# Gated mix of two attention blocks: all PSUM banks in one tile, with joined exponentials and row maxima and an own order per pair of key tiles

## The chip, the core and the metric

The kernel runs on one core of a Trainium2 chip. Its engines work side by side: TensorE (PE) multiplies matrices into PSUM, which has eight banks of 128 x 512 f32; VectorE (DVE) and ScalarE (ACT) read PSUM and write SBUF; GpSimd (POOL) works in SBUF; SyncE (SP) issues DMAs. Each engine runs its own instructions in order and waits for others through semaphores: each engine has a count that its finished instructions raise, and a wait names a count that has to be reached. The metric is the time of one execution on the device in microseconds, lower is better; before it is 2671.39 us, the median of three runs.

## The reference

Two attention blocks over the same x (2048 tokens, 576 features, 32 heads of 18) are mixed by a sigmoid gate. Block A has its own keys and values for each head, block B one key and one value head for all:

```python
g = sigmoid((x * gate_w).sum(-1, keepdims=True))
a = softmax(qA @ kA.T * 18**-0.5) @ vA @ A_wo        # per head, 32 heads
b = softmax(qB @ kB.T * 18**-0.5) @ vB @ B_wo        # one k, v for 32 heads
out = g * a + (1 - g) * b
```

B's query and key weights are drawn eight times larger than the others, so its scores are large and the row maxima are needed.

## The kernel before

There are 64 heads in all (`NU`, 32 of B, then 32 of A). A first stage projects x into queries, keys and values and parks them in DRAM; the values are still projected while the first maxima run. The main stage walks over `NSTEP` = 1024 steps, a step being one tile of 128 rows of one head, two steps (a **pair**) a turn of the loop over `T`, eight pairs a head.

Three streams run at once, at different places of the walk:

- **Maxima**, 22 steps ahead (`LEAD`). `step_max` multiplies 128 query rows with 512 keys (one chunk `c` of four) into a PSUM bank, and DVE takes the row maximum (L524). Chunks 0 and 1 share one DVE pass: a product with the difference of the two key chunks (`x`) goes through a Relu on ACT into SBUF (L518), and a custom DVE instruction adds it to chunk 0's product and takes the maximum (L521). So a step has four matmuls, three DVE passes and one ACT pass. `max_rows` gathers the maxima of a head and puts them into two more rows of the queries, through which the next product subtracts them.
- **Scores** at `T`. `step_scores` multiplies 128 keys with 512 queries (four chunks a step) into a bank, and ACT takes the exponential into an SBUF tile (L560).
- **PV**, one or two steps behind. `step_pv` multiplies the exponentials with the values, four chunks on four column groups, and adds up in the bank `acc` over 16 steps (L566), whole (512 columns) or in two halves of 256. `head_out` copies `acc` out once a head (L588).

The operands of scores lie in partitions 0 to 55, those of maxima and `x` in 64 to 117, so that two matmuls can be in the array at once.

PSUM is in three pools: four banks for scores and `x` (`ps_s`), three for maxima (`ps_m`), one for `acc`. Each call of a pool's `tile` gives the next buffer, and the framework makes a matmul wait for whoever read the buffer last. The exponentials have a pool of 12 buffers of 128 x 512.

The order on PE is written by hand: strings of operations, one for each pair, chosen by the place in the head (`PLAIN`, `END`, `AFTER`, `BEFORE_ROWS`, `ROWS`) and by whether a unit of the output projection is due (`UNIT`, `UNIT_END`, `UNIT2`). `mB1` is the maximum of the second step's chunk 1, `sA0` the score of the first step's chunk 0, `x` the difference product, `P` and `Q` a whole PV step, `p f` and `h H` its halves, `U` a unit (12 matmuls and an addition into `oacc`, L695 and L703). The order on ACT and DVE follows from it, since each consumer is recorded right behind its matmul. A turn of the loop:

```python
for op in order.split():
    k, second, c = op[0], op[1:2] == "B", op[2:]
    ...
    elif k in "mM":
        step_max(*divmod(M + second, 16), int(c), k == "M", T < 0 and c == "3")
    elif k == "s":
        ...
```

DMAs are issued beside this by SP, from generators (`normalise`, `prep_wo`, `out_proj`) that are pulled once a turn.

Of the kernel before, what the change touches and what calls it, by code (L numbers as in the profile page):

```python
# [19 lines left out]
S = 2048  # L20
D = 576
H = 32
# [27 lines left out]
def gated_mix_kernel(ctx: ExitStack, tc: tile.TileContext, xT, wall, wv, wo, out):  # L50
# [34 lines left out]
    ones_r = dram.tile([2, S], F16, name="ones_r")  # L85
    acc = ps_o.tile([P, 512], F32, name="acc")

    def other():
        return ps_s.tile([P, 512], F32, name="ps")

# [150 lines left out]
    def bank(odd=False):  # L241
        return ps_m.tile([P, 512], F32, name="pm") if odd else ps_s.tile([P, 512], F32, name="ps")

# [50 lines left out]
    def project_v(st_, hf, w):  # L294
        fp = ps_s.tile([P, 512], F32, name="ps")
# [206 lines left out]

    def step_max(u, i, c, low=False, spare=False):

# [7 lines left out]
        else:  # L512
            k = kst(u)[b:b + 54, c * 512:(c + 1) * 512]
        pm = other() if c == "x" or spare else ps_m.tile([P, 512], F32, name="pm")
        nc.tensor.matmul(pm, qs[u % 3][b:b + 54, i * P:(i + 1) * P], k, start=True, stop=True)  # L515
        if c == "x":
            MX["x", u, i] = lead.tile([P, 512], F32, name="xb", bufs=2)
            nc.scalar.activation(MX["x", u, i], pm, AF.Relu)  # L518
        elif c == 0 and ("x", u, i) in MX:
            junk = lead.tile([P, 512], BF16, name="junk", bufs=1)  # L520
            nc.vector.tensor_tensor_reduce(junk, pm, MX.pop(("x", u, i)), 1.0, -3e38, op0=OP.add, op1=OP.max,  # L521
                                           accum_out=MX[u][:, i, c:c + 1])
        else:
            nc.vector.tensor_reduce(MX[u][:, i, c:c + 1], pm, axis=AX.X, op=OP.max)  # L524
# [20 lines left out]

    def step_scores(u, i, c, alone, x=None):

        x = c if x is None else x
        b = SB
        ps = (ps_m if alone and c == 0 else ps_s).tile([P, 512], F32, name="pm" if alone and c == 0 else "ps")  # L550
        if alone and c % 2:
            b = MB
        nc.tensor.matmul(ps, kst(u)[b:b + 56, i * P:(i + 1) * P],  # L553
                         qs[u % 3][b:b + 56, x * 512:(x + 1) * 512], start=True, stop=True)
        PT["q"] = PT.get("q", []) + [(x, ps)]
        if alone and c == 0:
            return
        for c, ps in PT.pop("q"):
            pt = L["pt"].tile([P, 512], F32, name="pt")
            nc.scalar.activation(pt, ps, AF.Exp, scale=SCALE / LIFT ** 2)  # L560
            PT[u, i, c] = pt

# [105 lines left out]
    def out_proj(t0, rows, first=False):  # L668
# [15 lines left out]
        for q in range(8):  # L684
# [3 lines left out]
            for s2 in range(2):  # L688
                st_ = 2 * q + s2
                for hf in range(2):  # L690
                    fp = ps_m.tile([P, 512], F32, name="pm")
                    n = 0
# [23 lines left out]

    def end_bank(n=[0]):
        n[0] += 1
        return ps_s.tile([P, 512], F32, name="ps") if n[0] % 7 < 4 else ps_m.tile([P, 512], F32, name="pm")

    def last_half(h):
# [10 lines left out]
        yield  # L732
        pt = ps_m.tile([P, 512], F32, name="pm")[:, 0:256]
        for c in range(2):
# [7 lines left out]
        yield  # L742
        pb = ps_m.tile([P, 512], F32, name="pm")[:, 0:256]
        for c in range(2):
# [7 lines left out]
    def end_bank(n=[0]):  # L752
        n[0] += 1
        return ps_s.tile([P, 512], F32, name="ps") if n[0] % 7 < 4 else ps_m.tile([P, 512], F32, name="pm")

    def last_units():

        w = WO[8]
        for n in range(32):
            st_, hf = divmod(n, 2)  # L760
            end = END_T[st_ // 8]
            fp = end_bank() if n > 1 else ps_m.tile([P, 512], F32, name="pm")
            for m, (a, b) in enumerate(PRODS):
# [67 lines left out]

    FIRST = "sA0 mA2 sA1 mA0 sA2 mA3 sA3 mB0 sB0 mB1 sB1 mB2 sB2 mB3 sB3 x"
    PLAIN = "mB1 mB3 sA0 sA1 mA3 sA2 P mB2 sA3 x sB0 mA2 sB1 mB0 h sB2 mA0 H sB3"
    UNIT = "mB2 sA0 mB0 sA1 mA0 P mB3 sA2 mA2 sA3 Q mA3 sB0 x sB1 mB1 sB2 U sB3"
    END = "mB2 sA0 mB3 mB1 sA1 p sA2 mA2 sA3 mA0 sB0 f x mB0 sB1 mA3 sB2 Q sB3"
    AFTER = "mB1 mA3 sA0 sA1 sA2 mA0 P sA3 mA2 sB0 mB2 x sB1 mB0 h sB2 mB3 H sB3"
    BEFORE_ROWS = "mA0 sA0 mB3 sA1 mB1 sA2 p sA3 mA2 f sB0 mB2 sB1 mB0 x sB2 mA3 Q sB3"
    ROWS = "mB3 sA0 mA3 sA1 mB1 sA2 P mB2 sA3 sB0 mA0 x sB1 mB0 h sB2 mA2 H sB3"
    UNIT_END = "mB3 sA0 mA2 sA1 mA3 sA2 P sA3 mB1 sB0 mB2 Q x sB1 mA0 sB2 mB0 sB3 U"
    UNIT2 = "sA0 mA3 sA1 mB0 sA2 P sA3 mB1 sB0 mB2 sB1 x U mA2 sB2 mA0 sB3 Q mB3"  # L840
    ALONE = "sA0 sA1 P U sA2 sA3 U sB0 sB1 h U sB2 sB3 H U"
# [4 lines left out]
    LAST_U = (TL + 14,)  # L846
    LEADS = "mA0 MA1 mA2 MA3 V.A mB0 MB1 mB2 MB3 V.B"
    order = None
    TAIL = {TL: [N8], TL + 2: [N8], TL + 6: [N8, N8, N8], TL + 8: [HALF[0]], TL + 10: [N8]}
    for T in range(-LEAD, NSTEP + 2, 2):  # L850
# [9 lines left out]
        order = LEADS if T < 0 else FIRST if T == 0 else LAST if T > TL else ALONE if alone else (UNIT2 if T >= SEG[1][3] else UNIT_END if T % 16 == 0 else UNIT) if units else \  # L860
            {0: END, 2: AFTER if T > 2 else PLAIN, 8: BEFORE_ROWS, 10: ROWS}.get(T % 16, PLAIN)
        for op in order.split():
# [87 lines left out]
```

## Time and profile before

| what | us |
|---|---|
| median of three runs | 2671.39 |
| lowest and highest | 2669.41, 2672.8 |
| span of the profiled execution, first to last instruction | 2669.7 |
| busy: PE, DVE, ACT, POOL | 2652.4, 2421.4, 2393.3, 283.8 |

The profiled execution has no time of its own beside its span; the median of the runs lies 1.7 us above that span. Busy is the time in which at least one instruction of the engine is under way. A matmul's row begins when it starts and ends when its last result is in PSUM, while the next one starts earlier, so a busy PE need not be at its peak. Rows of the profile name line, engine, operation, output and input, and the count; in brackets stands how long the engine was idle before, and who ended that.

### The profile page before, as it was taken

How to read it: one execution, taken by the hardware profiler on the slowest of the kernel's cores; microseconds unless marked ns; L12 is line 12 of the kernel's file. 1: busy time of each engine (PE TensorE's matmuls, PEld its weight loads, DVE VectorE, ACT ScalarE, POOL GpSimd, SP SyncE). 2: the span in 40 equal slices, each digit the busy share in tenths (PEclk: the TensorE clock that was granted, in tenths of full speed). 3: DMA queues.
4: the chain of work that ended last, by engine and by line, in shares of the span. 5: the costliest groups of instructions: out<-in, count | busy, mean ns of one | idle time of the engine just before them, and what ended most of it. 6: DMA issues, size and time to landing. Idle time of an engine off the chain costs nothing.

```text
span 2669.7 us, 58607 instructions
## 1 busy us (share of the span) xinstructions
PE 2652.4 (99%) x22278; PEld 898.0 (34%) x22278; DVE 2421.4 (91%) x4588; ACT 2393.3 (90%) x4814; POOL 283.8 (11%) x526
## 2 busy tenths in 40 slices
PE   9999999999999999999999999999999999999998
PEld 7778322222222222222222222222222222223444
DVE  8447999999999999999999999999999999998873
ACT  4341899999999999999999999999999999998875
POOL 4740000001001100100110002000200011001000
PEclk9999999999999999999999999999999999999999
DMA  7332000011001100210132112112121212122312
GB/s 202 125 112 76 23 20 20 20 37 40 28 17 46 44 20 18 54 33 20 36 77 82 43 53 85 43 55 59 58 67 51 55 54 61 40 70 86 90 36 95
DMA packets 127304, 150.15 MB, mean 56 GB/s; under 512 B 55456, under 2 KB 94744, under 8 KB 125933
## 3 DMA queue, kind: packets, MB, share of 16 engines
q1 hardware_dynamic: 112593, 119.38, 15.7%
q0 software_dynamic: 8096, 19.30, 2.1%
q10 hardware_dynamic: 6332, 7.71, 0.8%
q8 instruction: 175, 2.87, 0.4%
q14 instruction: 108, 0.88, 0.1%
HBM read 90.80 MB, written 46.45 MB: 51 GB/s over the span
## 4 chain that ended last, share of the span: by engine, by line
PE 93%; DVE 5%; ACT 1%; DMA 1%; issue 1%; SPq 0%; ACTq 0%; DVEq 0%
PE acc L566 38%; PE ps L553 26%; PE pm L515 13%; PE pm L695 4%; PE ps L515 4%; PE ps L248 3%; PE pm L248 3%; DVE mx L524 2%; PE ps L297 2%; DVE junk L521 0%; ACT pt L560 0%; DVE norm_a L190 0%; DVE pl L262 0%; DMA R<-r_d 0%; DVE oacc L772 0%
## 5 line engine op out<-in xcount | busy, mean ns | idle before, releaser
L560 ACT ACTIVATE pt<-ps 128x512 f32<-128x512 f32 x4074 | 2105.6, 651 | 63.1 <-PE ps L553 51.5
L524 DVE TENSOR_REDUCE mx<-pm 128x1 f32<-128x512 f32 x3072 | 1914.1, 682 | 68.0 <-PE pm L515 34.0
L553 PE MATMUL ps<-qs,ksb 56*128 56x512 f16 x2688 | 807.3, 380 | 0.0
L515 PE MATMUL pm<-ksb,qs 54*128 54x512 f16 x2341 | 762.5, 380 | 1.1 <-DVE mx L524 0.6
L566 PE MATMUL acc<-pt,vb 128*19 128x256 f32 (+1 forms) x6144 | 592.4, 457 | 0.0
L566 PE MATMUL acc<-pt,vg 128*19 128x256 f32 (+1 forms) x5496 | 561.7, 480 | 0.3
L515 PEld LDWEIGHTS <-qs 54*128 54x128 f16 x4096 | 293.1, 94 | 516.1 <-issue 455.4
L553 PE MATMUL ps<-qs,ksa 56*128 56x512 f16 x1386 | 407.5, 380 | 0.3
L515 PE MATMUL pm<-ksa,qs 54*128 54x512 f16 x1232 | 399.8, 380 | 1.6 <-DVE mx L524 1.1
L553 PEld LDWEIGHTS <-ksb 56*128 56x128 f16 x2688 | 202.4, 93 | 487.5 <-issue 446.3
L521 DVE CUSTOM_DVE_ANT_0 junk<-pm,xb 128x512 bf16<-128x512 f32 x501 | 341.0, 681 | 9.4 <-PE pm L515 9.0
L518 ACT ACTIVATE xb<-ps 128x512 f32<-128x512 f32 x501 | 319.6, 638 | 7.7 <-PE ps L553 7.3
L534 POOL TENSOR_SCALAR mt<-mt 128x32 f32<-128x32 f32 x64 | 18.6, 290 | 1626.4 <-DVE mt L532 1626.4
L553 PEld LDWEIGHTS <-ksa 56*128 56x128 f16 x1408 | 100.6, 94 | 233.1 <-issue 213.5
L566 PEld LDWEIGHTS acc<-pt,vb 128*19 128x19 f32 x6144 | 104.3, 97 | 216.1 <-issue 208.6
L566 PEld LDWEIGHTS acc<-pt,vg 128*19 128x19 f32 x5496 | 93.2, 97 | 213.1 <-issue 209.7
L515 PE MATMUL ps<-kdb,qs 54*128 54x512 f16 x373 | 140.5, 377 | 0.1
L300 ACT ACTIVATE vst<-ps 128x288 f32<-128x288 f32 x32 | 13.2, 412 | 60.6 <-PE ps L297 60.6
L256 ACT ACTIVATE ph<-ps,tv 128x512 f16<-128x512 f32 x29 | 19.8, 687 | 49.3 <-PE ps L248 34.3
L256 ACT ACTIVATE ph<-pm,tv 128x512 f16<-128x512 f32 x27 | 18.3, 687 | 48.0 <-PE pm L248 29.4
L703 DVE TENSOR_TENSOR oacc<-pm,oacc 128x288 f32<-128x288 f32 x32 | 14.6, 457 | 46.0 <-PE pm L695 45.9
L262 DVE SCALAR_TENSOR_TENSOR pl<-pm,tv,ph 128x512 f16<-128x512 f32 x27 | 20.0, 748 | 37.5 <-ACT ph L256 24.5
(167 smaller groups left out, 1544.6 us busy)
## 6 DMA issues: line engine op xcount, KB each, us to landing
qs<-qkh SPq DMA_DIRECT2D x244, 72.0 KB
qs<-qkl SPq DMA_DIRECT2D x122, 72.0 KB
onh<-oh SPq DMA_DIRECT2D x32, 256.0 KB
onl<-ol SPq DMA_DIRECT2D x32, 256.0 KB
oih<-onh SPq DMA_DIRECT2D x16, 512.0 KB
oil<-onl SPq DMA_DIRECT2D x16, 512.0 KB
ot<-oe SPq DMA_DIRECT2D x220, 36.0 KB
qkh<-ph POOLq DMA_DIRECT2D x56, 128.0 KB, 2.1
```

The costliest lines, as they stand in the source:

```text
L248: nc.tensor.matmul(fp[:, a0:b0], w[a][:kr, k, :], X[b][:kr, k, s0 + a0:s0 + b0], start=(n == 0), stop=(n == len(PROJ) - 1), skip_group_che ...
L256: nc.scalar.activation(h, fp, AF.Copy, scale=t)
L262: nc.vector.scalar_tensor_tensor(l, fp, t, h, op0=OP.mult, op1=OP.subtract)
L297: nc.tensor.matmul(fp[:, 0:288], X[b][:kr, k, st_ * P:(st_ + 1) * P], w[a][:kr, k, :], start=(n == 0), stop=(n == len(PROJ) - 1))
L515: nc.tensor.matmul(pm, qs[u % 3][b:b + 54, i * P:(i + 1) * P], k, start=True, stop=True)
L518: nc.scalar.activation(MX["x", u, i], pm, AF.Relu)
L521: nc.vector.tensor_tensor_reduce(junk, pm, MX.pop(("x", u, i)), 1.0, -3e38, op0=OP.add, op1=OP.max, accum_out=MX[u][:, i, c:c + 1])
L524: nc.vector.tensor_reduce(MX[u][:, i, c:c + 1], pm, axis=AX.X, op=OP.max)
L553: nc.tensor.matmul(ps, kst(u)[b:b + 56, i * P:(i + 1) * P], qs[u % 3][b:b + 56, x * 512:(x + 1) * 512], start=True, stop=True)
L560: nc.scalar.activation(pt, ps, AF.Exp, scale=SCALE / LIFT ** 2)
L566: nc.tensor.matmul(acc[32 * j:32 * j + 19, a:b], v_of(u, i), PT[u, i, j][:, a:b], start=(i == 0 and a == 0), stop=(i == 15), skip_group_ch ...
L695: nc.tensor.matmul(fp[:, 0:288], o[b][:r, t, s2 * P:(s2 + 1) * P], w[a][:r, t, 288 * hf:288 * hf + 288], start=(n == 0), stop=(n == 3 * nt ...
```

## The change

PSUM becomes a single tile `bk` of eight banks. Two counters stand for the pools: `next_s` gives banks 0 to 3 in turn, `next_m` banks 4 to 6; `acc` is bank 7. The exponentials get one tile of 16 slots. A score that is held (`S` in the orders means: take this score's exponential together with the one before) is not given to ACT at once, and one ACTIVATE then reads two banks and writes two slots; of two maxima where the second is marked `N`, one DVE reduce reads two banks and writes two numbers. Where the two banks don't follow each other, the access takes them with a stride, in ascending order, as 0 and 3. The strings now name eight scores, six maxima, one chunk 0 (`c`) and one `x` a pair, with `p0` and `p1` for the two PV steps and `h` and `f` for a half and a whole, and there is one string for each of a head's eight pairs. Pairs with a unit have the same strings with `U` at the end. The turns ahead of `T` = 0 and behind the last maximum keep their old strings.

```diff
-    ps_s = ctx.enter_context(tc.tile_pool(name="ps_s", bufs=4, space=PSUM))
-    ps_m = ctx.enter_context(tc.tile_pool(name="ps_m", bufs=3, space=PSUM))
-    ps_o = ctx.enter_context(tc.tile_pool(name="ps_o", bufs=1, space=PSUM))
+    ps = ctx.enter_context(tc.tile_pool(name="ps", bufs=1, space=PSUM))
...
+    bk = ps.tile([P, 8, 512], F32, name="bk")
+    acc = bk[:, 7, :]
+    RING = {"s": 0, "m": 0}
+
+    def next_s():
+        RING["s"] += 1
+        return (RING["s"] - 1) % 4
+
+    def next_m():
+        RING["m"] += 1
+        return 4 + (RING["m"] - 1) % 3
...
-        L["pt"] = ctx.enter_context(tc.tile_pool(name="ppool", bufs=12, side="left"))
+        L["pt"] = ctx.enter_context(tc.tile_pool(name="ppool", bufs=1, side="left")).tile([P, 16, 512], F32, name="pt")
...
+        elif join == "first":
+            MX["j"] = (n, 4 * i + c)
+        elif join == "second":
+            (n0, c0), (n1, c1) = sorted((MX.pop("j"), (n, 4 * i + c)))
+            flat = MX[u].rearrange("p i c -> p (i c)")
+            nc.vector.tensor_reduce(flat[:, c0:c1 + 1:c1 - c0], bk[:, n0:n1 + 1:n1 - n0, :], axis=AX.X, op=OP.max)
...
+    def exps(q):
+
+        q = sorted(q, key=lambda e: e[0])
+        t = next_pt(len(q))
+        n = [e[0] for e in q]
+        if len(q) == 1:
+            o, i = L["pt"][:, t[0], :], bk[:, n[0], :]
+        else:
+            o, i = L["pt"][:, t[0]:t[1] + 1:t[1] - t[0], :], bk[:, n[0]:n[1] + 1:n[1] - n[0], :]
+        nc.scalar.activation(o, i, AF.Exp, scale=SCALE / LIFT ** 2)
...
-    PLAIN = "mB1 mB3 sA0 sA1 mA3 sA2 P mB2 sA3 x sB0 mA2 sB1 mB0 h sB2 mA0 H sB3"
...
-    AFTER = "mB1 mA3 sA0 sA1 sA2 mA0 P sA3 mA2 sB0 mB2 x sB1 mB0 h sB2 mB3 H sB3"
...
+    PLAIN = ("s c m x s N S p0h m s p0h m s m s S N s p1f",
+             "m s s N S s m p0f x s c S m p1h s m m s p1h",
+             "m s s m p0h x s c s s m p0h m S N s p1h s m p1h",
+             "s m m s S m s p0f s c m s m S p1h s m x p1h",
+             "s m m s S N s p0h s m p0h c s s m N S x p1f",
+             "s m s N S s m p0f s m x s m N S p1h s c p1h",
+             "m s m s m s p0h x s m s p0h s c S m m s p1f",
+             "m s m x s S N p0h c s p0h m s s m S m s p1f")
...
+        for n, op in enumerate(ops):
+            if op in "sS":
+                k = ns.index(n)
+                step_scores(*divmod(T + k // 4, 16), k % 4, hold=k < 7 and ops[ns[k + 1]] == "S")
```

What stands on PE at the start of a head's second pair. Names are tile and operand, `ps` a score's or an `x`'s bank, `pm` a maximum's, `bk` any bank of the new tile, and the bracket names the engine whose count is waited for. Before, L553 is a score, L515 a maximum, L566 PV:

```order
L515 LDWEIGHTS qs_94
L515 MATMUL pm<-ksb,qs_94 128x512 [waits DVE_49]
L553 LDWEIGHTS ksb
L553 MATMUL ps<-qs_93,ksb 128x512 [waits Activation_49]
L553 LDWEIGHTS ksb
L553 MATMUL ps<-qs_93,ksb 128x512 [waits Activation_49]
L553 LDWEIGHTS ksb
L553 MATMUL ps<-qs_93,ksb 128x512 [waits Activation_49]
L515 LDWEIGHTS qs_94
L515 MATMUL pm<-ksb,qs_94 128x512 [waits DVE_49]
L566 MATMUL acc<-pt,vb 19x512 [waits DVE_49]
L566 MATMUL acc<-pt,vb 19x512 x3
```

and after, where L588 is a score, L527 a maximum and L603 PV, from the pair's second score (held, bank 3) over its joined score (bank 0) and the next one (bank 1) to PV:

```order
L588 LDWEIGHTS ksb
L588 MATMUL bk<-qs_87,ksb 128x512
L527 LDWEIGHTS qs_88
L527 MATMUL bk<-ksb,qs_88 128x512 [waits DVE_49]
L588 LDWEIGHTS ksb
L588 MATMUL bk<-qs_87,ksb 128x512
L588 LDWEIGHTS ksb
L588 MATMUL bk<-qs_87,ksb 128x512 [waits Activation_49]
L527 LDWEIGHTS qs_88
L527 MATMUL bk<-ksb,qs_88 128x512
L603 MATMUL bk<-pt,vb 19x512 [waits DVE_49]
L603 MATMUL bk<-pt,vb 19x512 x3
```

followed, behind that PV step, by:

```order
L527 LDWEIGHTS qs_88
L527 MATMUL bk<-kdb,qs_88 128x512
L588 LDWEIGHTS ksb
L588 MATMUL bk<-qs_87,ksb 128x512
L527 LDWEIGHTS qs_88
L527 MATMUL bk<-ksb,qs_88 128x512 [waits DVE_49]
L588 LDWEIGHTS ksb
L588 MATMUL bk<-qs_87,ksb 128x512
L527 LDWEIGHTS qs_88
L527 MATMUL bk<-ksb,qs_88 128x512
```

Before, each score waits for ACT by itself. After, the scores into banks 3 and 0 carry no wait; the one into bank 1 does, ahead of PV; of the later matmuls the `x` (bank 2) and the scores into banks 3 and 0 carry none again.

On ACT, around the same pair, L560 and L518 of before are an exponential and an `x`'s Relu:

```order
L518 ACTIVATE xb<-ps 128x512 [waits DVE_49,PE_49]
L560 ACTIVATE pt<-ps 128x512 [waits PE_49] x8
L518 ACTIVATE xb<-ps 128x512 [waits DVE_49,PE_49]
L560 ACTIVATE pt<-ps 128x512 [waits PE_49] x7
L518 ACTIVATE xb<-ps 128x512 [waits DVE_49,PE_49]
```

and after, L577 and L530 are those:

```order
L577 ACTIVATE pt<-bk 128x512 [waits PE_49,Activation_49]
L577 ACTIVATE pt<-bk 128x1024 [waits PE_49,Activation_49]
L577 ACTIVATE pt<-bk 128x512 [waits PE_49]
L530 ACTIVATE xb<-bk 128x512 [waits DVE_49,PE_49]
L577 ACTIVATE pt<-bk 128x1024 [waits PE_49,Activation_49]
L577 ACTIVATE pt<-bk 128x512 [waits PE_49]
L577 ACTIVATE pt<-bk 128x512 [waits PE_49,Activation_49] x3
L530 ACTIVATE xb<-bk 128x512 [waits DVE_49,PE_49]
```

Seven or eight exponentials between two Relus were as many instructions, with one wait each; in the piece of after two instructions write 1024 columns, and several also wait for ACT's own count, for the older exponential in the same slots.

More of the change, by code (lines that the diff above doesn't have):

```diff
@@ L294, in project_v @@
     def project_v(st_, hf, w):
-        fp = ps_s.tile([P, 512], F32, name="ps")
+        fp = other()
         for n, (a, b, k, kr) in enumerate(PROJ):
@@ L501, in gated_mix_kernel, with step_max @@
     MX = {}
-    def step_max(u, i, c, low=False, spare=False):
+    def step_max(u, i, c, low=False, spare=False, join=None):
         if u not in MX:
@@ L847, in gated_mix_kernel, with steps_pair @@
     LEADS = "mA0 MA1 mA2 MA3 V.A mB0 MB1 mB2 MB3 V.B"
+    def steps_pair(T, M, order, units):
+        ops = order.split()
+        ns = [n for n, op in enumerate(ops) if op in "sS"]
+        nm = [n for n, op in enumerate(ops) if op in "mN"]
+        ncm = [n for n, op in enumerate(ops) if op == "c"]
+        maxima = [(0, c) for c in range(2, 4)] + [(1, c) for c in range(4)]
+        assert len(ns) == 8 and len(nm) == 6 and len(ncm) == 1
+        which = {}
+        for k, n in enumerate(nm):
+            which[n] = maxima[k]
+        ring = RING["m"]
+        at_bank = {}
+        for n, op in enumerate(ops):
+            if op in "mNcU":
+                at_bank[n] = ring % 3
+                ring += 1
+        joined = {n for k, n in enumerate(nm) if k + 1 < len(nm) and ops[nm[k + 1]] == "N"}
+        for k, n in enumerate(nm):
+            if ops[n] == "N" and at_bank[nm[k - 1]] > at_bank[n]:
+                which[n], which[nm[k - 1]] = which[nm[k - 1]], which[n]
+        for n, op in enumerate(ops):
+            if op in "sS":
+                k = ns.index(n)
+                step_scores(*divmod(T + k // 4, 16), k % 4, hold=k < 7 and ops[ns[k + 1]] == "S")
+            elif op in "mN":
+                e, c = which[n]
+                step_max(*divmod(M + e, 16), c, join="second" if op == "N" else "first" if n in joined else None)
+            elif op == "c":
+                step_max(*divmod(M, 16), 0)
+            elif op == "x":
+                if M + 2 < NSTEP:
+                    step_max(*divmod(M + 2, 16), "x")
+            elif op == "U":
+                pull(1)
+            elif T >= 2:
+                k, h = int(op[1]), op[2]
+                part = PART.get(k, 0)
+                PART[k] = part + (256 if h == "h" else 512)
+                step_pv(*divmod(T - 2 + k, 16), part, PART[k])
+                if PART[k] == 512:
+                    del PART[k]
+                    if k == 1 and T % 16 == 0:
+                        head_out(T // 16 - 1)
+    PART = {}
     order = None
```

70 lines of the change are left out of this document (40 added, 30 removed), and 7 rows, old and new, of the table UNIT2.

## The prediction

> **What bounds the kernel now.** I read the page first, then the copies that end each head, then one head's stretch, then its chain. The page's span, its busy line and its chain by engine:
>
> ```profile
> span 2669.7 us, 58607 instructions
> PE 2652.4 (99%) x22278; PEld 898.0 (34%) x22278; DVE 2421.4 (91%) x4588; ACT 2393.3 (90%) x4814; POOL 283.8 (11%) x526
> PE 93%; DVE 5%; ACT 1%; DMA 1%; issue 1%; SPq 0%; ACTq 0%; DVEq 0%
> ```
>
> PE carries the chain. The copy of the accumulator (L588) runs once a head; three answers on its line (count, least/median/most ns, first and last start) give the period of a head in three parts of the program, and one stretch of a head's length shows the engines:
>
> ```profile
> L588 DVE COPY oe<-acc x28: 680/681/682, 316.4 to 1277.4; 128x512 f32<-128x512 f32 x28
> L588 DVE COPY oe<-acc x22: 681/686/686, 1456.0 to 2250.0; 128x512 f32<-128x512 f32 x22
> L588 DVE COPY oe<-acc x4: 684/685/686, 2430.3 to 2569.9; 128x512 f32<-128x512 f32 x4
> 387.50:423.00 35.50, 35.50 (x322) 9.12 (x320) 35.13 (x68) 35.46 (x73) 0.75 (x3) 1.00 0.07 19
> ```
>
> A plain head takes (1277.4 - 316.4) / 27 = 35.59 us, a head with projection units 794.0 / 21 = 37.81, one of the last 139.6 / 3 = 46.53. In the stretch PE, DVE (35.13) and ACT (35.46) are all full, so what PE must do and what it waits for have to be told apart. The chain of waits, piece by piece (start, length), does that:
>
> ```profile
> 423.43 0.21 PE ps L553
> 423.64 0.20 PE pm L515
> 423.84 0.01 PE ps L553
> 423.85 0.98 PE acc L566 x8
> 424.84 0.32 PE ps L553
> 425.16 0.00 PE pm L515
> 425.16 0.21 PE ps L553
> ...
> 425.93 0.56 PE acc L566 x8
> 426.49 0.32 PE ps L553
> 426.80 0.01 PE pm L515
> 426.81 0.56 PE acc L566 x8
> ```
>
> A score and a maximum on different rows of the array run side by side and cost one slot of 0.215 us, 0.32 behind a PV group; a whole PV step costs 0.98, a half 0.56. A head of before has 24 groups of 72 slots (each string gone through, two of the same kind taking two slots), 16 halves, 8 wholes: 24 x 0.32 + 48 x 0.215 + 16 x 0.56 + 8 x 0.98 = 34.8 us. PE waits 0.8 us a head, no more: it is the bound, with the two others close behind.
>
> **The change, part by part: the work.** The new strings have 25 groups, 70 slots, 18 halves and 7 wholes: 8.0 + 45 x 0.215 + 18 x 0.56 + 7 x 0.98 = 34.62 us of PE, 0.18 less. For ACT and DVE, the spacing of single instructions and what 512 more elements cost:
>
> ```profile
> 1000.25 4.03 ACT L560 ACTIVATE pt<-ps 128x512 f32<-128x512 f32 x8
> 437.32 2.48 DVE L524 TENSOR_REDUCE mx<-pm 128x1 f32<-128x512 f32 x4
> L136 ACT ACTIVATE wh<-wst 128x512 fp32r<-128x512 f32 x14 | 8.7, 624 | 3.9 <-DMA wst<-wall 3.9
> L339 ACT ACTIVATE xh<-xs 128x1024 fp32r<-128x1024 f32 x8 | 8.4, 1056 | 0.5 <-DMA xs<-xT 0.4
> L177 DVE TENSOR_REDUCE norm_b<-wst 128x1 f32<-128x512 f32 x3 | 2.0, 673 | 0.0
> L177 DVE TENSOR_REDUCE norm_b<-wst 128x1 f32<-128x312 f32 x1 | 0.5, 459 | 0.0
> L560 ACTq EVENT_SEMAPHORE  x31: 17/17/17, 350.1 to 1418.2; - x31
> ```
>
> Exponentials follow each other at (4.03 - 0.65) / 7 = 0.48 us; a second bank adds 1056 - 624 = 432 ns, so a joined pair takes 0.91 instead of 0.96. Not shown is a read of two PSUM banks: the second could cost from 0.43 (this row) to 0.48 (a whole one more); I take 0.43, the only row of that length. 14 joins a head save up to 0.7 us of ACT. Against it, an exponential that also waits for an older one needs a separate wait of 17 ns; the built program has 756 more, 12 a head, 0.2 us. Reduces follow at (2.48 - 0.68) / 3 = 0.60, a second bank adds 512 x 214 / 200 = 548 ns, so a join saves 0.05; the built program has 9 a head, 0.5 us. None of this is on PE. If PE were free of new waits, a head would take between 34.62 and, with the 0.8 us of waits kept, 35.4 us.
>
> **The waits.** All of PSUM is one tile now, and the built program takes a strided access as covering everything between its ends. A join of banks 0 and 3 counts as touching 1 and 2. In the second pair of a head (the PE rows shown with the change) the ring stands so that the held score and the one joined to it fill banks 3 and 0; the next score, bank 1, waits for ACT's count 1408, and the instruction that raises it to 1408 is the exponential of 0 and 3. Bank 1's own reader stood two instructions earlier. The later rows agree: the matmuls into banks 2, 3 and 0 carry no wait, though the join has just read 3 and 0, since that one wait covers them. Of 875 joined exponentials 375, six a head, are 0 with 3; of 562 joined maxima 196, three a head, are 4 with 6, and the next matmul into bank 5 waits for them alike. PE is in order, so all behind the waiting matmul stands still, PV steps too.
>
> The price comes from three delays of before: a matmul to the exponential that waits for it, an exponential's length, and its end to the matmul that waits (the same for a reduce):
>
> ```profile
> 583.21 0.39 PE L553 MATMUL ps<-qs,ksb 56*128 56x512 f16 x1
> 583.63 1.08 ACT L560 ACTIVATE pt<-ps 128x512 f32<-128x512 f32 x2 [0.16 <-PE pm L515]
> 276.29 0.60 ACT L560 ACTIVATE pt<-ps 128x512 f32<-128x512 f32 x1 [0.40 <-PE pm L515]
> 276.94 0.37 PE L553 MATMUL ps<-qs,ksb 56*128 56x512 f16 x1
> 275.83 0.69 DVE L524 TENSOR_REDUCE mx<-pm 128x1 f32<-128x512 f32 x1 [0.35 <-PE pm L515]
> 276.58 0.37 PE L515 MATMUL pm<-ksb,qs 54*128 54x512 f16 x1 [0.17 <-DVE mx L524]
> ```
>
> That is 0.42, 0.60 and 276.94 - 276.89 = 0.05. From the start of the score that completes a join to the start of the score that waits for it at least 0.42 + (0.60 + 0.43) + 0.05 = 1.50 us pass. In four of the six places the waiting matmul is the next slot, 0.215 after: 1.28 us lost each, 5.14 in all. In one a slot and a half PV step lie between, 0.215 + 0.32 + 0.56 = 1.10, lost 0.40; in one a half PV step, 0.88, lost 0.62. Sum 6.16 us a head. For a join of 4 and 6 it is 0.42 + 0.69 + 0.55 + 0.06 = 1.72; over the nine places, less what lies between and what an exponential's wait covers already, 3 x 0.84 + 0.62 + 0.21 + 0.22 = 3.57, and a third of them in each head falls on 4 and 6: 1.2 us. Its bounds are 0, if those waits fall under others, and 3 x 0.84 = 2.5.
>
> PE's head becomes 34.62 + 6.16 + 1.2 = 41.98. Of the 0.8 us of old waits I keep half, 0.4, since ACT and DVE now have some 8 us a head to catch up in: 42.4, or 6.8 us over 35.59. Its ends: 40.8 with no DVE waits and no old ones, 44.3 with the old ones whole and each join begun 0.25 us late behind an ACT still at work (6 x 0.25). Joins occur from the second pair on until the maxima end, 500 pairs or 62.5 heads; I take the same loss in heads with units, where PE has the same strings and the unit on top. 62.5 x 6.8 = 425 us, on the span 2669.7: 3095. The runs' median is 1.7 us above that execution's span: **3096 us**. The larger ring of exponentials costs and hides nothing: PV reads two pairs behind, and its rows have no wait on ACT.
>
> **Rivals.** *The other side: the bank waits are already met.* If the exponential of 0 and 3 ended before PE came to bank 1, only the smaller work would count: 34.62 to 35.4 us a head, 62.5 x -0.2 to -1.0, that is 2610 to 2660, say 2640. For it: all three engines have less to do. Against it: the waited-for exponential cannot begin until the score just ahead of the waiting one is done; it turns only where over 1.28 us of PE work lies between those two, and in four of six places none does.
>
> *The clock falls.* Two pauses of 1.28 us lie 1.7 us apart, at the end of the fifth pair of a head and in the sixth. The windows (PE busy, ..., granted clock, DMA share, GB/s) show two falls of before:
>
> ```profile
> 66.00:70.00 4.00, 2.49 (x12) 1.77 (x11) 3.39 (x8) 0.00 (x0) 2.88 (x4) 1.00 0.29 98
> 72.00:75.00 3.00, 3.00 (x9) 2.37 (x9) 1.41 (x2) 1.12 (x2) 1.93 (x4) 0.58 0.23 79
> 276.00:279.00 3.00, 2.62 (x12) 0.81 (x10) 3.00 (x7) 2.71 (x6) 0.00 (x0) 1.00 0.20 66
> 279.00:283.00 4.00, 3.96 (x17) 0.69 (x17) 2.92 (x5) 3.28 (x7) 0.00 (x0) 0.57 0.00 0
> ```
>
> With PE busy 2.49 of 4 us, and 2.62 of 3, the clock fell to a half for some (1 - 0.57) / 0.5 x 4 = 3.4 us. Of a new head of 42.4 us about 29 are matmuls at work (70 slots of 0.215, 16 PV steps less their change-over), two thirds; at half speed a spell loses about 3.4 / 2 x 0.68 = 1.15 us. Once a head: 62.5 x 1.15 = 72 us, 3168; three times, 3310. Against it: by far the most of a head has pauses further apart than these two. [...]
>
> *Half the price.* If only the exponentials' waits bit and the old waits vanished, 40.8 us a head: 62.5 x 5.2 = 325, 2996. This is the low end of the forecast.
>
> *The change does not join what it says.* The built program has 875 and 562 joins over 62.5 heads: it does.
>
> **How the numbers follow.** Forecast, full clock, 2996 to 3215 (44.3 us a head): 0.74. Clock falls, 3168 and up: 0.14. Waits already met, 2610 to 2660: 0.06. Something cancels the waits to within a measurement: 0.02. Slower by under 300 us through a cause I don't see: 0.04. From 2980 to 3240 lies the forecast and half of the clock case, 0.81. A measurement of this kernel tells some 0.2% from no change: faster 0.06, same 0.02, slower 0.92.
>
> **What would show it.** Right: the accumulator copies stand 41 to 44 us apart; in the second pair of a head a score starts 1.5 us behind the one before it, 0.05 behind a joined exponential of some 1.03 us; the same twice in the fifth to sixth and in the eighth pair; ACT's and DVE's busy shares fall under 85% and exponentials wait for PE; places that join neighbouring banks show none of it. Wrong: heads of 35 us or less, or scores into bank 1 that start beside the joined exponential; a granted clock under 1.0 within the heads would be the clock's case.

## The result and the profile after

The changed kernel takes 3259.22 us (median of four runs, 3256.24 to 3261.41), 1.2205 times the time of before, 95% interval [1.2187, 1.2222]. That is 163 us more than predicted and 19 over the range's upper end. The page of its profiled execution, span, busy line and chain by engine:

```profile
span 3254.5 us, 59842 instructions
PE 2805.2 (86%) x23238; PEld 967.0 (30%) x23238; DVE 2448.0 (75%) x4026; ACT 2423.9 (74%) x3939; POOL 282.8 (9%) x526
PE 61%; ACT 23%; DVE 12%; issue 3%; DMA 0%; POOL 0%; SPq 0%; ACTq 0%; DVEq 0%; POOLq 0%
```

No engine is full any more, and ACT and DVE, which had 1% and 5% of the chain, hold 35%: the engines wait for each other in turn. The copies that end a head (now L625; count, least/median/most ns, first and last start) of the plain heads, of the heads with units and of three of the last:

```profile
L625 DVE COPY oe<-bk x32: 691/692/693, 332.9 to 1712.6; 128x512 f32<-128x512 f32 x32
L625 DVE COPY oe<-bk x21: 691/692/694, 1756.8 to 2709.4; 128x512 f32<-128x512 f32 x21
L625 DVE COPY oe<-bk x4: 691/691/692, 2974.6 to 3149.0; 128x512 f32<-128x512 f32 x4
```

A plain head takes 1379.7 / 31 = 44.51 us (35.59 before), one with units 952.6 / 20 = 47.63 (37.81), one of the last 58.1 (46.53). The chain of waits (start, length), at the place in the head's second pair of which the prediction spoke:

```profile
1000.15 0.02 PE bk L588
1000.17 0.02 issue
1000.19 0.02 ACTq L577
1000.21 0.04 issue
1000.25 0.38 ACT pt L577
1000.63 0.11 issue
1000.75 1.03 ACT pt L577
1001.77 0.04 issue
1001.82 0.37 PE bk L588
```

The held score and its partner are done; ACT first takes an earlier exponential (1000.25), then the joined one (1000.75, 1.03 us), and 0.05 us behind its end the score into bank 1 starts. Six places of that head as the timeline has them, the bracket being how long PE stood idle and for whom, with the row of the joined score (the second of two) first; two are in the second pair, one is a joined maximum's, two lie at the fifth and sixth pairs, one in the eighth:

```profile
999.99 0.59 PE L588 MATMUL bk<-qs,ksb 56*128 56x512 f16 x2
...
1001.82 0.37 PE L588 MATMUL bk<-qs,ksb 56*128 56x512 f16 x1 [1.23 <-ACT pt L577]
...
1005.11 0.37 PE L588 MATMUL bk<-qs,ksb 56*128 56x512 f16 x1 [0.61 <-ACT pt L577]
...
1010.67 0.37 PE L527 MATMUL bk<-ksb,qs 54*128 54x512 f16 x1 [0.44 <-DVE mx L540]
...
1020.44 0.37 PE L527 MATMUL bk<-kdb,qs 54*128 54x512 f16 x1 [1.13 <-ACT pt L577]
...
1023.78 0.37 PE L588 MATMUL bk<-qs,ksb 56*128 56x512 f16 x1 [1.23 <-ACT pt L577]
...
1042.44 0.37 PE L588 MATMUL bk<-qs,ksb 56*128 56x512 f16 x1 [1.26 <-ACT pt L577]
```

The joined score starts at 999.99 + 0.59 - 0.37 = 1000.21, so 1.61 us pass to the waiting one where the prediction had 1.50. The list of waits sums them (us in total, times, longest):

```profile
PE bk L588 <- ACT pt L577: 292.5, 287, 2.3
PE bk L527 <- ACT pt L577: 71.1, 62, 1.2
PE bk L527 <- DVE mx L540: 69.1, 118, 1.3
```

and the groups by form have the joined instructions (busy us, mean ns):

```profile
L577 ACT ACTIVATE pt<-bk 128x1024 f32<-128x1024 f32 x875 | 898.8, 1027 | 4.1 <-PE bk L588 3.3 <-PE bk L527 0.3
L540 DVE TENSOR_REDUCE mx<-bk 128x2 f32<-128x1024 f32 x562 | 685.7, 1220 | 122.4 <-PE bk L527 118.5 <-PE bk L588 1.6
```

The rows with ACT as the releaser count 349 waits, which is close to the 375 strided joins. A joined exponential lasts 1.03 us and a joined reduce 1.22, as worked out (1.03 and 0.69 + 0.55 = 1.24). The strided read itself is hardly slower: the shortest of the 875 joined exponentials lasts 1017 ns, so with a mean of 1027 the 375 strided ones among them last at most 1.04 us in the mean; and the 366 joined reduces of e1 below, all of neighbouring banks, last 1214 ns in the mean, against 1220 here with 196 strided ones among 562.

### The profile page after: what moved, and what is told of

The parts are those of the page before. It is cut to its first block, busy times and chain, and to the rows that moved or that the text cites. A ratio compares the mean times of both kernels' runs of the same rounds, so it can differ in the third digit from the quotient of the medians.

```text
span 3254.5 us, 59842 instructions
## 1 busy us (share of the span) xinstructions
PE 2805.2 (86%) x23238; PEld 967.0 (30%) x23238; DVE 2448.0 (75%) x4026; ACT 2423.9 (74%) x3939; POOL 282.8 (9%) x526
## 4 chain that ended last, share of the span: by engine, by line
PE 61%; ACT 23%; DVE 12%; issue 3%; DMA 0%; POOL 0%; SPq 0%; ACTq 0%; DVEq 0%; POOLq 0%
PE bk L603 24%; ACT pt L577 20%; PE bk L527 14%; PE bk L588 12%; PE bk L259 5%; DVE mx L542 4%; DVE mx L540 4%; PE bk L732 4%; ACT xb L530 2%; DVE junk L533 2%; PE bk L308 2%; DVE sm L654 0%; DVE oacc L805 0%; PE bk L797 0%; SPq L56 0%
## 5 line engine op out<-in xcount | busy, mean ns | idle before, releaser
L577 ACT ACTIVATE pt<-bk 128x512 f32<-128x512 f32 (+1 forms) x3221 | 2103.6, 720 | 465.4 <-PE bk L588 274.1
L542 DVE TENSOR_REDUCE mx<-bk 128x1 f32<-128x512 f32 x1970 | 1264.9, 684 | 261.8 <-PE bk L527 191.0
L588 PE MATMUL bk<-qs,ksb 56*128 56x512 f16 x2688 | 826.5, 387 | 193.6 <-ACT pt L577 193.6
L527 PE MATMUL bk<-ksb,qs 54*128 54x512 f16 x2363 | 746.8, 386 | 46.9 <-DVE mx L540 45.8
L540 DVE TENSOR_REDUCE mx<-bk 128x2 f32<-128x1024 f32 x562 | 685.7, 1220 | 122.4 <-PE bk L527 118.5
L603 PE MATMUL bk<-pt,vb 128*19 128x256 f32 (+1 forms) x6400 | 617.2, 458 | 0.2 <-PE bk L527 0.2
L603 PE MATMUL bk<-pt,vg 128*19 128x256 f32 (+1 forms) x6200 | 592.2, 454 | 0.0
L527 PEld LDWEIGHTS <-qs 54*128 54x128 f16 x4096 | 288.4, 94 | 748.2 <-issue 687.9
L588 PE MATMUL bk<-qs,ksa 56*128 56x512 f16 x1408 | 419.2, 384 | 99.2 <-ACT pt L577 98.9
L533 DVE CUSTOM_DVE_ANT_0 junk<-bk,xb 128x512 bf16<-128x512 f32 x501 | 345.8, 690 | 129.5 <-PE bk L588 80.4
L527 PE MATMUL bk<-ksa,qs 54*128 54x512 f16 x1232 | 392.8, 382 | 23.6 <-DVE mx L540 23.3
L530 ACT ACTIVATE xb<-bk 128x512 f32<-128x512 f32 x501 | 300.2, 599 | 80.8 <-PE bk L527 49.3
L588 PEld LDWEIGHTS <-ksb 56*128 56x128 f16 x2688 | 205.0, 94 | 425.0 <-issue 360.7
L603 PEld LDWEIGHTS bk<-pt,vb 128*19 128x19 f32 x6400 | 109.2, 97 | 397.4 <-issue 396.7
L603 PEld LDWEIGHTS bk<-pt,vg 128*19 128x19 f32 x6200 | 105.5, 97 | 374.2 <-issue 373.9
L527 PE MATMUL bk<-kdb,qs 54*128 54x512 f16 x373 | 143.6, 385 | 52.8 <-ACT pt L577 52.8
L588 PEld LDWEIGHTS <-ksa 56*128 56x128 f16 x1408 | 103.8, 94 | 213.4 <-issue 174.8
L625 DVE COPY oe<-bk 128x512 f32<-128x512 f32 x63 | 43.6, 692 | 102.2 <-PE bk L603 102.2
```

The lines of the kernel that those rows point to most:

```text
L540: nc.vector.tensor_reduce(flat[:, c0:c1 + 1:c1 - c0], bk[:, n0:n1 + 1:n1 - n0, :], axis=AX.X, op=OP.max)
L577: nc.scalar.activation(o, i, AF.Exp, scale=SCALE / LIFT ** 2)
L588: nc.tensor.matmul(bk[:, n, :], kst(u)[b:b + 56, i * P:(i + 1) * P], qs[u % 3][b:b + 56, x * 512:(x + 1) * 512], start=True, stop=True)
L603: nc.tensor.matmul(acc[32 * j:32 * j + 19, a:b], v_of(u, i), PT[u, i, j][:, a:b], start=(i == 0 and a == 0), stop=(i == 15), skip_group_ch ...
L625: nc.vector.tensor_copy(oe, acc)
```

## The experiments

"W" is the prediction's cause: the framework takes an access over banks 0 and 3 (or 4 and 6) as one that covers the banks between, and PE waits for the joined reader. All times have the kernel before, run beside them on the same chip, as the base of the ratio.

**e1: joins of neighbouring banks alone.** The strings, tile and rings stay; a pair that isn't in neighbouring banks is read by two single instructions.

```diff
+            if n1 - n0 > 1:
+                for b0, f0 in (j, (n, 4 * i + c)):
+                    nc.vector.tensor_reduce(flat[:, f0:f0 + 1], bk[:, b0, :], axis=AX.X, op=OP.max)
+            else:
...
-        if alone:
+        if alone or len(q) == 2 and abs(q[0][0] - q[1][0]) > 1:
```

> The changed kernel, but a held score whose banks are 0 and 3, and a pair of maxima in banks 4 and 6, are read one bank at a time; 500 of 875 exponentials and 366 of 562 maxima stay joined. Theory W (a joined access over banks that don't touch is taken to cover the banks between, and PE waits for it): nothing is left to wait for, a plain head takes 35 to 35.6 us, the clock stays full, 2640 to 2720 us in all. Rival J (a read of two banks is itself what costs, by holding two banks to its end): 500 + 366 of 1437 joins are left, so some 60% of the 588 us stay, about 3020. Rival O (the order of the strings costs): no change, about 3250.

Measured: 2691.45 us, ratio 1.0079 [1.0062, 1.0096]. Its busy line, and the copies of its plain heads:

```profile
PE 2668.0 (99%) x23238; PEld 954.8 (35%) x23238; DVE 2388.7 (89%) x4222; ACT 2372.0 (88%) x4314; POOL 283.4 (11%) x526
```

```profile
L630 DVE COPY oe<-bk x32: 678/679/681, 322.6 to 1425.0; 128x512 f32<-128x512 f32 x32
```

Its chain by line from 1000 to 1040 us, and all of PE's waits for DVE's maxima:

```profile
by line: PE bk L608 48.1%; PE bk L527 29.8%; PE bk L593 22.8%
```

```profile
PE bk L527 <- DVE mx L545: 1.5, 8, 0.2
PE bk L527 <- DVE mx L547: 1.1, 4, 0.5
```

Of the 588 us that the change lost (3259.22 - 2671.25, before in the same runs), 568 go with the strided joins. A plain head is 1102.4 / 31 = 35.56 us, and its chain is PE and nothing else. 500 joined exponentials and 366 joined maxima are still there, so joining and holding a score cost nothing to speak of where the banks are neighbours.

**e2: only the strided exponentials undone**, so that the 196 strided maxima remain.

```diff
-        if alone:
+        if alone or len(q) == 2 and abs(q[0][0] - q[1][0]) > 1:
```

> The changed kernel with the exponentials of banks 0 and 3 read one bank at a time, the maxima of banks 4 and 6 still joined (196 of them, three a head). W: the run with neighbours only plus 62.5 x 1.2 = 75 us, at most plus 155. J: about 3100, O: about 3250.

**e3: only the strided maxima undone**, so that the 375 strided exponentials remain.

```diff
-            nc.vector.tensor_reduce(flat[:, c0:c1 + 1:c1 - c0], bk[:, n0:n1 + 1:n1 - n0, :], axis=AX.X, op=OP.max)
+            if n1 - n0 > 1:
+                for b0, f0 in (j, (n, 4 * i + c)):
+                    nc.vector.tensor_reduce(flat[:, f0:f0 + 1], bk[:, b0, :], axis=AX.X, op=OP.max)
```

> The changed kernel with the maxima of banks 4 and 6 read one bank at a time, the exponentials of banks 0 and 3 still joined (375, six a head). W: 6.2 us a head of waits are left, 62.5 x 6.2 = 385 us above the run with neighbours only, and some falls of the clock with them: 3070 to 3190. J and O: 3200 or more.

Measured: e2 2846.50 us, ratio 1.0661 [1.0639, 1.0682]; e3 3173.61, ratio 1.1886 [1.1862, 1.1909]. PE's wait in e2, then PE's waits in e3:

```profile
PE bk L527 <- DVE mx L540: 116.1, 171, 1.4
```

```profile
PE bk L593 <- ACT pt L582: 304.4, 308, 2.3
PE bk L527 <- ACT pt L582: 69.8, 62, 1.1
```

and the copies of two plain heads of e3 in a row:

```profile
L630 DVE COPY oe<-bk x3: 691/692/693, 984.1 to 1068.9; 128x512 f32<-128x512 f32 x3
```

Each kind of join makes its own wait and leaves the other's out. Alone, the maxima cost 155 us over e1, twice the 75 of the prediction and just what was expected at most; on top of the exponentials they cost 3259 - 3174 = 86. The exponentials alone cost 482, in which are the falls of the clock that come with them (e3's mean clock is 0.976).

**e4: the ring moved by one.** The score counter starts at 3, and nothing else changes: 125 joins instead of 375 now fall on banks 0 and 3.

```diff
-    RING = {"s": 0, "m": 0}
+    RING = {"s": 3, "m": 0}
```

> The changed kernel with the score banks' counter begun at 3 instead of 0 and nothing else: as many joins, but 125 of them (two a head) instead of 375 on banks 0 and 3. W: of 6.16 us a head the two places left cost 1.28 + 0.62 = 1.9, so 62.5 x 4.26 = 266 us less than the changed kernel, more if the clock falls less often: 2920 to 3000. J and O: no change, about 3250, since joins, strings and counts of instructions are the same.

Measured: 2950.84 us, ratio 1.1051 [1.1029, 1.1073]. PE's waits:

```profile
PE bk L588 <- ACT pt L577: 116.4, 126, 2.1
PE bk L527 <- DVE mx L540: 93.6, 122, 1.4
```

The order, the number of joins and the work are those of the changed kernel; only the bank under each join is another. The waits for ACT fall from 349 to 126, and the joins that span the gap from 375 to 125. With e2's strided maxima as base, 104 us are left for those 125. This is the strongest run for W: which banks a join reads decides.

**e5: no join at all**, with the changed strings.

```diff
-                step_scores(*divmod(T + k // 4, 16), k % 4, hold=k < 7 and ops[ns[k + 1]] == "S")
+                step_scores(*divmod(T + k // 4, 16), k % 4, hold=False)
...
-                step_max(*divmod(M + e, 16), c, join="second" if op == "N" else "first" if n in joined else None)
+                step_max(*divmod(M + e, 16), c, join=None)
```

> The strings, the one tile, the rings and the 16 slots of the changed kernel, with no join at all: 4813 exponentials and 3195 reduces of 512 each. Against it stands the kernel that joins neighbouring banks only (span 2690.9, plain heads 35.56 us). Theory W (all of the loss is the waits of the strided joins, and what the joins save lies on ACT and DVE, which PE does not wait for): 2685 to 2705, plain heads within 0.2 us of 35.56. Rival J+ (the joins of neighbouring banks hide a part of the strings' own cost, since ACT and DVE are nearly full and a join takes 0.02 to 0.05 us less): 2715 to 2740, heads 0.5 to 0.7 us longer. Rival J- (a join costs, since its bank comes free later): 2670 to 2680.

Measured: 2702.58 us, ratio 1.0119 [1.0104, 1.0133]; a plain head 35.80. The time lies in theory W's range, the head 0.04 us above it: joins of neighbours do bring something, 0.24 us a head or 11 us in all, less than half of what J+ wanted.

**e6: unit pairs with two whole PV steps**, on top of e1.

```diff
-        return (UNIT2[k // 2] if T >= SEG[1][3] else UNIT[k]) if units else PLAIN[k // 2]
+        return "m s m s c p0f m s m s p1f m s x s m s U s" if units else PLAIN[k // 2]
```

> The kernel with joins of neighbouring banks only, but the pairs with a projection unit have a string of their own with two whole PV steps in place of one whole and two halves or four halves. By the slots of the prediction a half taken away from a step saves 2 x 0.56 - 0.98 = 0.14 us and a group's 0.32 - 0.215. Theory U (the unit heads are longer than before, 38.27 against 37.79 us, because their strings have lost the whole PV steps): unit heads 37.2 to 37.9, the whole 2665 to 2685. Rival D (the unit heads are bound by DVE, which adds the unit up, so that the string on PE does not matter): unit heads 38.1 to 38.5, the whole 2688 to 2695.

Measured: 2690.86 us, ratio 1.0076 [1.0062, 1.0091], against 1.0079 of e1. The heads with units take 38.37 us (e1 38.27), so theory U falls for them. The last heads, where every pair has a unit, fall from 47.94 to 46.58, before's 46.53. D's numbers hold, but not its reason. PE's list of waits for the unit stretch has 0.6 us for DVE, and the windows of that stretch (length, then busy time and instructions of PE first), of e6 and of e7 below, whose unit heads are as short as before's, show PE full in both:

```profile
1460.70:2228.00 767.30, 765.29 (x6682) 232.79 (x6680) 706.02 (x1267) 725.45 (x1320) 53.65 (x99) 1.00 0.20 55
```

```profile
1461.60:2217.80 756.20, 755.53 (x6522) 219.24 (x6520) 714.15 (x1345) 728.97 (x1470) 53.61 (x99) 1.00 0.20 56
```

PE has 160 matmuls more over 20 heads, eight a head: one more piece of a PV step, though the units' own strings are as before's. By the prediction's slots that is some 0.14 us (2 x 0.56 - 0.98) and 0.1 for a group more, of the 0.56 that the heads are longer; the rest stays open.

**e7: the strings of before in one tile**, rings by hand, 16 slots, no joins.

```diff
-    ps_s = ctx.enter_context(tc.tile_pool(name="ps_s", bufs=4, space=PSUM))
...
+    ps = ctx.enter_context(tc.tile_pool(name="ps", bufs=1, space=PSUM))
...
+    bk = ps.tile([P, 8, 512], F32, name="bk")
...
-            pt = L["pt"].tile([P, 512], F32, name="pt")
+            pt = L["pt"][:, RING["pt"] % 16, :]
+            RING["pt"] += 1
```

> The strings of before and no joins, but PSUM as one tile, the rings by hand and the 16 slots for exponentials. Theory T (the tile, rings and slots cost nothing by themselves, and what the kernel with neighbouring joins loses against before lies in its strings): 2664 to 2678, plain heads 35.4 to 35.7 us. Rival R (the one tile makes waits of its own, and the 16 slots hide nothing): 2685 to 2700, the same loss as that of the kernel with neighbouring joins.

Measured: 2676.91 us, ratio 1.0023 [1.0014, 1.0033]. Theory T's range holds, but the tile isn't quite free. A plain head is 35.61 us, as before; nearly all of the loss is made ahead of the first copy. The same product of the first stage in the timeline of before and of e7:

```profile
30.39 1.20 PE L248 MATMUL ps<-xh,wh 128*128 128x512 f32 x4 [0.67 <-ACT xh L339]
```

```profile
33.75 1.65 PE L253 MATMUL bk<-xh,wh 128*128 128x512 f32 x3 [3.65 <-DVE pl L267]
```

e7's first copy comes at 321.7 us, before's at 316.4:

```profile
L594 DVE COPY oe<-bk x63: 679/682/692, 321.7 to 2618.1; 128x512 f32<-128x512 f32 x63
```

Before, this product waits for its operand and not for a bank. That fits a pool that gave the bank of a small early product (the mask's) out again at once, since it was free; then it wasn't the plain ring that the section on the kernel before makes of it. No trace names the bank, but e9 tests it. The ring by hand goes on to the next bank, whose reader DVE is late by 3 us.

That is only a part. In e7 the first score of the main stage starts at 278.11 us and the first exponential at 281.08, before at 275.38 and 276.29: the lag of 2.7 us grows to 4.8. The timeline has a second wait there, and PE stands still behind it for 2.0 us:

```profile
281.08 4.03 ACT L566 ACTIVATE pt<-bk 128x512 f32<-128x512 f32 x8 [2.46 <-DMA v_d<-vst]
```

ACT waits for a DMA out of `vst`, a buffer of the first stage; before's first exponential waits for PE alone. The changed kernel and the nine other runs, all with the tile of 16 slots, have this wait too, of 2.30 to 2.73 us. That the tile lies where such a buffer was, so that its first use waits for the buffer's last reader, is likely and not shown: no run has the one PSUM tile with separate buffers for the exponentials.

**e8: every pair with two whole PV steps**, no joins, meant to free PE.

```diff
-        return (UNIT2[k // 2] if T >= SEG[1][3] else UNIT[k]) if units else PLAIN[k // 2]
+        return "m s m s c p0f m s m s p1f m s x s m s U s" if units else "m s m s c p0f m s m s p1f m s x s m s s"
```

> No joins; every pair behind the first, with or without a unit, has one string with two whole PV steps (16 groups of 72 to 80 slots and 16 wholes a head, no halves). By the slots of the prediction PE's work falls from 34.62 to about 16 x 0.32 + 56 x 0.215 + 16 x 0.98 = 32.8 us a head. Theory A (PE is freed, and ACT and DVE become the bound at some 34.7 to 35.2 us a head): 2610 to 2660, with ACT or DVE carrying a good part of the chain. Rival B (a whole PV step of 0.98 us in one piece leaves ACT and DVE without new banks for longer than the rings hold, and they lose what PE gains): 2690 to 2800, heads of 36 us and more, with PE waiting for ACT or DVE behind each PV step.

Measured: 2881.36 us, ratio 1.0789 [1.0773, 1.0804]; a plain head 39.35 (e5 35.80). The time is 81 us above even B's range, the head within B's "36 us and more". Behind a PV step, in the timeline:

```profile
999.99 1.05 PE L608 MATMUL bk<-pt,vb 128*19 128x512 f32 x8
...
1001.43 0.60 ACT L582 ACTIVATE pt<-bk 128x512 f32<-128x512 f32 x1 [0.40 <-PE bk L593]
...
1002.08 0.37 PE L593 MATMUL bk<-qs,ksb 56*128 56x512 f16 x1 [0.28 <-ACT pt L582]
...
1002.57 0.37 PE L593 MATMUL bk<-qs,ksb 56*128 56x512 f16 x1
```

ACT runs dry during the PV step (0.40 us idle). Then the four banks are full, and PE's scores come at ACT's pace, 0.49 us apart instead of 0.215. So B's mechanism holds and its size doesn't: less work on PE, and a longer head. The halves in the strings are what keeps ACT and DVE fed.

**e9 and e10: the bank of the mask used again.** e9 does so on e7; e10 on e1, with e6's string in the last heads alone and the counter put right again at `T` = 0, so that the joins fall on the same banks as in e1.

```diff
         pt = other()
+        RING["s"] -= 1
```

> The strings of before in one tile with rings by hand and no joins, but the small product of the mask in the first stage gives its bank back, so that the next product takes the same bank again, as the pool of before did. Theory F (the 5.4 us by which the first accumulator copy comes late with the one tile come from the first stage, where a product that took the bank of the mask now takes the next bank and waits 3.6 us for its reader): first accumulator copy back at 327 to 329 us, the whole 2668 to 2673, within 0.2% of before. Rival G (the one tile itself, not the choice of the bank, makes the 5.4 us): first copy at 332 to 334, the whole 2675 to 2679.

> The kernel with joins of neighbouring banks only (2691), with the mask's bank used again as above, and with two whole PV steps in the unit pairs of the last stretch alone, where that string took the last heads from 47.94 to 46.58 us. By theory F and the last heads 2691 - 5.4 - 3 x 1.36 = 2681, or 2677 to 2685. If the gains don't add up (the heads take up what came early, as ACT and DVE are still nearly full): 2686 to 2691.

Measured: e9 2673.99 us, ratio 1.0013 [1.0004, 1.0022], between the ranges of F and G; its first copy comes at 319.5 us, 2.2 earlier than e7's and 3.1 behind before's. (The copy times in the expectation, 327 to 334, are some 11 us later than the copies of before and e7 that they stand for, 316.4 and 321.7; only their distance of 5 us can be compared.) e10 2685.55 us, ratio 1.0058 [1.0046, 1.0071]; last heads 46.60, first copy no earlier than e1's.

The traces tell the two parts of e7's lag apart. e9's first score starts at 275.87 us, 0.5 behind before's: F's wait is nearly all gone, though PE waits 1.8 us for a reader of the same kind at a later small product. What is left is the other part, the first exponential:

```profile
279.10 4.03 ACT L567 ACTIVATE pt<-bk 128x512 f32<-128x512 f32 x8 [2.71 <-DMA v_d<-vst]
```

So F explains a bit under half of the 5.3 us, and the first exponential's wait most of the rest. In e10 the mended bank doesn't help: PE waits 3.1 us at the later product, and the first score comes 1.6 us behind e1's (278.94 against 277.30). So of e10's two gains only that of the last heads arrives. No version here beats the kernel before; e9 comes within 0.13% of it.

## Why the prediction was right in its mechanism and wrong in its size

**Right.** The direction, the cause and the places. The waits stand where the second pair, the fifth to sixth and the eighth were said to have them, behind a joined exponential of 1.03 us, and PE starts 0.05 us after its end. Places with neighbouring banks show none (e1), and with a third of the joins on banks 0 and 3 a third of the waits for ACT is left (e4). DVE and ACT fell to 75% and 74%. The rivals "already met" and "does not join" fall with e1 and e3.

**Wrong: the size, 585 us on the span instead of 425.** The step that failed is the clock: the sum puts it at nothing ("Forecast, full clock"), which was the author's estimate and which no run of the changed kernel shows, and leaves it to a rival with a chance of 0.14. The profiled run shows a mean granted clock of 0.973, worth some 55 us. Without these the time would have been about 3204, inside the range. Three other terms were too small as well. By the terms of the sum, for a plain head (42.4 us forecast, 44.51 measured):

- *PE's work and the old waits*, 34.62 + 0.4 = 35.02. e1, without strided joins, has 35.56. What failed here is "PE waits 0.8 us a head": it was a difference between a head and a sum of slots. In e1 PE's idle time for DVE's maxima is 2.6 us in the whole program. The rest was mostly work that the slots undercounted, and it didn't go away: 0.5 us. (A wait of under some 0.15 us would not show as idle time, since a matmul's row of 0.37 outlasts its slot of 0.215; how much of the 0.5 is that stays open.)
- *The exponentials' places*, 6.16. In e3 two heads take 84.8 us, 42.4 each, so 6.9 over e1; that the clock is full in them is an estimate, from their being 1.1 us shorter than e3's plain heads in the mean, (1677.0 - 328.4) / 31 = 43.50. The 1.50 us was written down as "at least" and then used as the value. The joined exponential starts 0.54 us after its score (1000.75 - 1000.21) rather than 0.42, because an earlier exponential is still in front of it on ACT. At the five places of that head where the wait ends with an exponential, the joined ones start 0.02 to 0.27 us later than that 0.42, 0.7 together.
- *The maxima's places*, 1.2 on top of the others. Three heads of the changed kernel at a granted clock of 1.00 (first row below) take 130.3 / 3 = 43.43, which is 1.0 over e3's: close. Alone they cost double (e2), since the prediction's sum counts only what an exponential's wait doesn't cover.
- *The clock*, nothing in the forecast, 0.14 as a rival. Between the plain heads' 44.51 and the 43.43 at full clock lie 1.1 us; 0.1 of it is no clock, since four of these 31 heads have some 0.8 us of other work more (the head from 1269.71 takes 44.77 at a granted clock of 1.00, its like 43.97). So the clock is 1.0 us a head, the largest miss in the plain heads. The copies of the three heads, and the mean granted clock of the core:

```profile
L625 DVE COPY oe<-bk x4: 691/692/693, 377.4 to 507.7; 128x512 f32<-128x512 f32 x4
```

```profile
core 0: 3254.5 us, clock 0.973
```

The windows (length; PE, PEld, DVE, ACT and POOL busy; granted clock, DMA share, GB/s) of two heads with the same joins, and of two falls:

```profile
685.88:729.91 44.03, 36.69 (x330) 9.64 (x330) 35.73 (x58) 36.18 (x58) 6.96 (x9) 1.00 0.13 39
951.23:999.86 48.63, 40.56 (x330) 10.02 (x330) 36.77 (x59) 36.60 (x58) 5.58 (x8) 0.89 0.17 39
...
968.00:972.00 4.00, 2.11 (x20) 0.60 (x17) 3.25 (x6) 2.37 (x5) 0.46 (x1) 1.00 0.05 14
972.00:976.00 4.00, 3.42 (x14) 0.59 (x14) 1.34 (x3) 1.49 (x3) 0.74 (x3) 0.52 0.03 4
...
544.00:548.93 4.93, 3.11 (x28) 0.67 (x25) 4.12 (x6) 3.83 (x6) 0.00 (x0) 1.00 0.08 24
548.93:552.34 3.41, 3.41 (x14) 0.58 (x14) 1.06 (x2) 1.19 (x2) 0.00 (x0) 0.50 0.02 5
```

The head of 48.63 us has 0.11 / 0.5 x 48.63 = 10.7 us at half clock, and it is one of the four with 0.8 us more of other work: (48.63 - 44.03 - 0.8) / 10.7 = 0.36 us lost for each us at half clock. A mean clock of 0.973 over the span is 0.027 / 0.5 x 3254.5 = 176 us at half; e1's 0.996 is 22 by the same working, so that some 154 are new and cost about 55 us by that rate, an estimate. The rival had 72 for one spell a head: its price for a us at half clock (1.15 / 3.4 = 0.34) was nearly right and its chance too low, and by its own sign, a granted clock under 1.0 within the heads, it came in on top of the forecast's waits. Its argument against itself looked at one place, the two pauses in the fifth and sixth pairs. Of the 26 falls in the main stage 22 begin at the eighth pair, as the one at 548.93 does, behind a pause of 0.56 to 0.86 us and one of 1.26 (once 1.54), with 1.7 of work between them; the sum had priced both (0.62 and 1.28) without setting them side by side. The fall at 972 begins inside the first of the rival's two pauses, with a pause of 1.26 for a joined maximum, which the rival left out, just ahead. The cost is read from heads of one run; no run took the clock's falls away while keeping the waits.

- *"The same loss in heads with units"*: 47.63 - 37.81 = 9.8 us instead of 6.8. Some 0.5 of it is there without strided joins (e1 38.27), the rest are the terms above, the clock among them, and a part that no run resolves. The last heads lost 11.6; 1.4 of it is the whole PV steps that their strings no longer have (e6).

Over 36 plain heads, 21 with units and 3 last ones the excesses of 2.1, 3.0 and 4.8 us make 76 + 63 + 14 = 153 of the 160 us. The one tile and the larger ring of exponentials were taken to cost nothing; e7 has 6 us, nearly all ahead of the first copy, and some 2 of these go with the first exponential's wait. No run shows a gain from the 16 slots.

## What to carry to other kernels

Where several banks become one tile, look up what the framework takes a strided access to cover before the order is planned: here a reader of the first and last bank made the writer of the banks between wait, and only joins of neighbours were free of that. A saving on engines that don't carry the chain is worth little (0.24 us a head here) against one wait on the engine that does (1.2 us a place). When a forecast puts new pauses on PE, price the granted clock in the forecast itself, from the few us where the pauses of all kinds lie densest and not from their mean distance.

## What the runs showed of the hardware beyond that

The clock fell to half without a long idle stretch ahead. From 968 to 972 us PE was busy for 2.11 of 4 us, and from 972 to 976 the mean granted clock was 0.52. PE's two pauses there, and the neighbouring stretch ahead of them:

```profile
969.69 0.37 PE L527 MATMUL bk<-ksb,qs 54*128 54x512 f16 x1 [1.26 <-DVE mx L540]
972.58 0.58 PE L527 MATMUL bk<-kdb,qs 54*128 54x512 f16 x1 [1.20 <-ACT pt L577]
```

```profile
965.00:968.00 3.00, 3.00 (x34) 0.77 (x26) 3.00 (x7) 3.00 (x6) 0.00 (x0) 1.00 0.02 5
```

Neither pause is over 1.3 us, and PE was busy throughout the 3 us ahead.

What the falls of this run have in common can be read from the trace's own list of them. The changed kernel has 29 within its span. They last 3.41, 6.83 or 10.24 us, at a granted clock of 0.50 (the one from 548.93 to 552.34 above), and their starts lie on one grid of 3.413 us, to within 5 ns: 548.93 and 637.67 are 26 steps of it apart. If the whole span is cut along this grid, the stretches at full clock in which PE is busy for less than 60% are followed by half clock in 24 of 27 cases, those with 60 to 64% in 5 of 97, and of the 777 with more none. The head at 685.88 has the same joins as the one at 951.23 and no fall: in the emptiest stretch of the one PE is busy for 2.11 of 3.41 us (from 705.92), in that of the other for 1.69 (from 968.77), and the clock falls at its end. In e4, with a third of the strided exponentials, the mean clock is 0.997, and in e3, with all of them and none of the strided maxima, 0.976. That the busy share of such a stretch is what sets the clock is the author's estimate from these counts. No run was made to test it, and the trace of before has a fall at 279.31 us (0.50 up to 282.72) behind a stretch in which PE is busy for 3.04 of 3.42 us.
